# Result stores of a fused attention and max-out kernel: from SyncE's DMA queue to GpSimd's

## The chip, the cores and the metric

The kernel runs on one core of one Trainium2 chip. The time is the device time of one execution, in microseconds (us), from the start of the program to its end. A change of 0.2% of it is 1.2 us.

The engines are named as in the profile: PE is TensorE (its matmuls; PEld its weight loads), DVE is VectorE, ACT is ScalarE, POOL is GpSimd, SP is SyncE, which here issues DMA transfers only. SPq stands for SP's instructions that issue transfers. All engines run side by side, each in the order of its own instruction list, and wait for one another through semaphores.

## The reference

Linear attention over 8 batches of 8 heads (576 rows, head size 64), and a max-out feed-forward over its result (4608 rows of 512, inner size 768), all in float32:

```python
q_s = softmax(q, axis=-1);  k_s = softmax(k, axis=2)      # the reference writes them out
kv  = np.einsum('bhsd,bhse->bhde', k_s, v)
x   = np.einsum('bhsd,bhde->bhse', q_s, kv)               # then rows of all heads side by side: 4608 x 512
h   = np.maximum(np.maximum(x @ w1, x @ w2), x @ w3)
out = h @ w_out
```

## The kernel before

A float32 product is made of three products of two-part operands (a high part and a rest), all summed in PSUM. A chunk is 512 rows of x. Chunk 0 goes through plain products. After it the chunks are taken in pairs, c = 1, 3, 5 and 7 (chunk 7 is paired with the leftover 64 rows of all batches), and a pair goes through seven products P1 to P7 in place of eight (Strassen's scheme in Winograd's form) in both layers.

The first layer of a pair (class `Duo`, `products`, PE L1393) runs over nine units u; a unit's order on PE is P1, P5, P4 of the unit before, P6, P2, P3, P7, each six matmuls of 512 columns. Three things pass between a unit's products through ACT: the copy of P1's sum into a second PSUM bank (`seeded`, L1448), which P6 and P2 add to; the copy of P5's sum into the SBUF tile s5 (L1441, `s_166` in instruction lists), after which P3 may start in P5's bank; and the copy of P6's sum into u2 (L1441, `u_167`), after which P7 may start. The weights of a product come by a transfer of 256 KB each (tiles ws, L1360).

The second layer of a pair (`second`, PE L1581) leaves, for each of v = 0 and 1, four result tiles of 128x512 (function `rows`): two are copied to a tile m of a pool of three (`alone`, L1606), two are summed in place (`added`, DVE L1611) in tiles that the next pair needs again. These are s6 and s7 (`s_164`, `s_165`) and s5 and u2. So the first layer of the next pair (c + 2) waits for stores of this pair: the copy into s5 and the copy into u2 of its unit 0 wait until the stores of these tiles have landed; and one of its seven operands, xb[3] (`xb_123`, cast by ACT at L1323), lies over s6 and waits for the store of s6. Each result is stored by one transfer of 256 KB: the inner function `store`, L1599.

The operands of a pair are made by ACT and DVE (L1323, L1325, L1329), now and then by POOL. POOL also sums weights (`mix_of`, L1235, tiles bd and bdf; L1247) and makes maxima over the partitions (L776, a custom instruction).

All instructions are recorded by one planner (class `Streams`) in a fixed sequence, the table `ORDER`. Each word names a stream and, with a letter, an engine; its step is appended to the instruction list of the engine that issues it. So a step's place among the instructions of its engine is fixed by its place in the table. Semaphore waits are added from the data that instructions share. A transfer takes the next of eight semaphores of its kind in turn and waits for the one that had it before. The program reserves 256 bytes of each SBUF partition as scratch for transfers whose descriptors software writes (L1965, `dynamic_dma_scratch_size=256`); the kernel before issues none such: all its transfers go through SP's queue, except one of ACT.

Of the kernel before, what the change touches and what calls it, by code (L numbers as in the profile page):

```python
# [156 lines left out]
def dve(n):  # L157
    return (n + 68) / 960
# [10 lines left out]
def act_psum(n):  # L169
    return n / 1300 + 0.086  # L170
# [154 lines left out]
def linear_attention_then_maxout_ffn(  # L325
# [29 lines left out]
    nc = tc.nc  # L355
    B, H, S, D = 8, 8, 576, 64
# [930 lines left out]
    class Duo:  # L1287
# [299 lines left out]
        def rows(self, v):  # L1587
            c, bank = self.c, self.bank
            s1, s5v = self.s1[v], self.s5[v]

            def copied(on, f, after, gives, take=()):
                yield Step("A", act_psum(CH), after, gives=("Y2", c, gives, v) if gives else None, take=take, rank=-1000.0)
                if take:
                    bank[on] = pf.tile([P, CH], F32, name="pf")
                    nc.scalar.copy(out=bank[on], in_=f)
                else:
                    nc.scalar.copy(out=f, in_=bank[on])

            def store(h, r, o, free=()):  # L1599
                yield Step("S", 0.42, kb=(128, 2048), gives=("out", c, r, h, v), free=free, rank=-1000.0)  # L1600
                nc.sync.dma_start(out=out_turned[c - 1 + h, 2 * v + r], in_=o)

            def alone(on, h, r, after, free):
                yield Step("A", act_psum(CH), after, take=[("tmp", (c, "y", v, r))], free=[free], rank=-1000.0)
                o = tmp.tile([P, CH], F32, name="m")
                nc.scalar.copy(out=o, in_=bank[on])  # L1606
                yield from store(h, r, o, [("tmp", (c, "y", v, r))])

            def added(on, f, r, after, gives, free=()):
                yield Step("V", dve(CH), after, gives=("Y2", c, gives, v), free=free)  # L1610
                nc.vector.tensor_tensor(out=f, in0=bank[on], in1=f, op=ALU.add)  # L1611
                yield from store(1, r, f)

            y = lambda i: ("pf", (c, "y", i + v))
            return [
                copied(("a", v), s1, [("Y", c, "P1", v), *self.room_s], "s1"),
                copied(("c", v), s5v, [("Y", c, "P5", v), ("out", c - 2, 1, 1, v) if c >= PAIRED else None], "s5"),
                alone(("a", v), 0, 0, [("Y", c, "P2", v), ("Y2", c, "s1", v)], y(0)),
                copied(("b", v), s1, [("Y2", c, "s1", v)], "seed", take=[y(4)]),
                copied(("b", v), s1, [("Y", c, "P6", v)], "u2"),  # L1620
                added(("b", v), s5v, 1, [("Y", c, "P7", v), ("Y2", c, "s5", v)], "c22"),
                added(("c", v), s1, 0, [("Y", c, "P3", v), ("Y2", c, "u2", v)], "c12", [y(2)]),
                alone(("b", v), 0, 1, [("Y", c, "P4", v)], y(4)),
            ]
# [222 lines left out]
    for c, ch in enumerate(chunks):  # L1847
        r = GATES_AT + 100.0 * c
# [11 lines left out]
    for n, d in enumerate(duos):  # L1860
        r = GATES_AT + 100.0 * (PAIRED + 2 * n)
# [18 lines left out]
    for n, d in enumerate([*duos, first]):  # L1880
        r = GATES_AT + 100.0 * (PAIRED + 2 * n)
# [97 lines left out]
```

## Time and profile before

| What | Value |
|---|---|
| Median of 3 runs | 610.97 us (610.48 to 611.84) |
| The profiled execution's own time | 610.54 us |
| Its span, first to last instruction | 608.7 us |
| PE busy | 599.1 us, 98% |
| DVE, ACT, POOL busy | 462.6, 352.1, 62.8 us |
| Result stores by L1601, 256 KB each | 32 on SP's queue |

The span leaves out 1.8 us of the profiled execution, ahead of the first instruction and behind the last. An engine's busy time says how much of the span it had an instruction under way; issuing a transfer is not counted as busy. The rows below give, for one place in the program, when each engine's instructions ran and what ended an idle time before them.

### The profile page before, as it was taken

The numbers are of one execution on the slowest core, as the hardware profiler recorded it, in microseconds if no ns is written. First come the engines' busy times: TensorE is split into PE (matmuls) and PEld (weight loads), VectorE is DVE, ScalarE is ACT, GpSimd is POOL, SyncE is SP. The second block draws the span as 40 slices with busy tenths as digits, with TensorE's granted clock in tenths as the row PEclk, the third lists the DMA queues.
The fourth block names the chain that finished last, engine by engine and source line by source line (L and its number), as shares of the span: only waits on it lengthen the run. The fifth ranks groups of instructions, "written<-read, shape, count | busy, mean of one in ns | idle before, by whom it ended". The sixth has DMA issues, their size and how long they took to land.

```text
span 608.7 us, 9795 instructions
## 1 busy us (share of the span) xinstructions
PE 599.1 (98%) x3359; PEld 482.8 (79%) x3359; DVE 462.6 (76%) x673; ACT 352.1 (58%) x881; POOL 62.8 (10%) x53
## 2 busy tenths in 40 slices
PE   6999999999999999999999999999999999999997
PEld 6688778778878777888787778888878788888886
DVE  8999999989999999955776987376558753242683
ACT  5999968776665696763664874222435641223271
POOL 1201212011201412300020000100010010000000
PEclk9999999999999999999999999999999999999999
DMA  8987789899899999999899846779777266666534
GB/s 318 403 315 248 284 296 367 252 305 320 287 303 326 350 292 278 349 301 294 304 269 303 259 117 204 222 202 288 214 200 226 88 188 191 190 211 214 148 96 146
DMA packets 67408, 154.75 MB, mean 254 GB/s; under 512 B 7712, under 2 KB 18592, under 8 KB 63776
## 3 DMA queue, kind: packets, MB, share of 16 engines
q1 hardware_dynamic: 67216, 154.07, 77.7%
q8 instruction: 27, 0.44, 0.3%
q14 instruction: 21, 0.17, 0.1%
q10 hardware_dynamic: 144, 0.07, 0.0%
HBM read 109.28 MB, written 37.75 MB: 242 GB/s over the span
## 4 chain that ended last, share of the span: by engine, by line
PE 95%; DVE 4%; DMA 1%; issue 0%; ACT 0%
PE pf L1393 50%; PE pf L1581 19%; PE pf L1096 15%; PE pf L1169 3%; PE pa L798 3%; PE pa L1005 2%; DVE qm L848 1%; DMA ident<-in_unit_matrix_dram 1%; PE sm L823 0%; PE pa L934 0%; DVE km L719 0%; DVE wx L587 0%; DVE wx L580 0%; DVE qe L866 0%; PE pa L978 0%; DVE qs L889 0%
## 5 line engine op out<-in xcount | busy, mean ns | idle before, releaser
L1393 PE MATMUL pf<-xb,ws 128*128 128x512 f32 x1134 | 259.9, 390 | 0.0
L1393 PEld LDWEIGHTS pf<-xb,ws 128*128 128x128 f32 x1134 | 212.4, 188 | 44.4
L1096 PE MATMUL pf<-x,wa 128*128 128x512 f32 x408 | 99.2, 396 | 0.0
L1096 PEld LDWEIGHTS pf<-x,wa 128*128 128x128 f32 x408 | 75.4, 188 | 18.6 <-issue 2.1
L1427 DVE TENSOR_TENSOR mm<-pf,mm 128x512 f32<-128x512 f32 x44 | 30.0, 686 | 61.6 <-PE pf L1393 61.4
L1448 ACT COPY pf<-pf 128x512 f32<-128x512 f32 x32 | 18.3, 572 | 93.3 <-PE pf L1393 87.5
L876 ACT ACTIVATE qt<-qt,qm 128x64 f32<-128x64 f32 x162 | 54.1, 338 | 3.6 <-DVE qm L872 2.1
L1441 ACT COPY u<-pf 128x512 f32<-128x512 f32 x27 | 15.8, 587 | 41.3 <-PE pf L1393 38.6
L876 ACT ACTIVATION_READ_ACCUMULATOR qt<-qt,qm 128x1 f32 x162 | 30.8, 190 | 0.0
L1518 DVE TENSOR_TENSOR mm<-mm 128x512 f32<-128x512 f32 (+1 forms) x32 | 29.9, 951 | 0.2
L776 POOL PARTITION_ALL_REDUCE kma<-km x12 | 14.4, 1199 | 138.4 <-DVE km L772 114.4
L1581 PE MATMUL pf<-op_a,oh 128*128 128x512 f32 x84 | 25.9, 389 | 0.0
L1581 PE MATMUL pf<-mix,so 128*128 128x512 f32 x84 | 25.3, 397 | 0.0
L1441 ACT COPY s<-pf 128x512 f32<-128x512 f32 x27 | 15.9, 587 | 15.8 <-PE pf L1393 14.3
L1323 ACT CAST xb<-xf 128x1024 fp32r<-128x1024 f32 x18 | 18.8, 1052 | 9.6 <-DVE xf L1329 6.0
L1433 DVE TENSOR_TENSOR mm<-pf,u 128x512 f32<-128x512 f32 x9 | 6.2, 690 | 21.4 <-PE pf L1393 21.4
L1325 DVE TENSOR_TENSOR xb<-xf,xb 128x1024 fp32r<-128x1024 f32 x16 | 19.9, 1251 | 3.0 <-ACT xb L1323 3.0
L1606 ACT COPY m<-pf 128x512 f32<-128x512 f32 x16 | 9.4, 585 | 18.7 <-PE pf L1581 18.7
L1581 PEld LDWEIGHTS pf<-mix,so 128*128 128x128 f32 x84 | 15.8, 188 | 3.7
L1581 PEld LDWEIGHTS pf<-op_a,oh 128*128 128x128 f32 x84 | 15.8, 188 | 3.3
L1514 DVE TENSOR_TENSOR op_a<-mm,op_a 128x1024 fp32r<-128x1024 f32 (+1 forms) x14 | 13.7, 983 | 5.4 <-ACT op_a L1512 5.4
L798 PEld LDWEIGHTS pa<-vt,kt 128*64 128x64 f32 x480 | 14.7, 137 | 3.2 <-issue 2.1
(248 smaller groups left out, 1126.8 us busy)
## 6 DMA issues: line engine op xcount, KB each, us to landing
ws<-keep_s SPq DMA_DIRECT2D x108, 256.0 KB, 3.9
ws<-keep_a SPq DMA_DIRECT2D x81, 256.0 KB, 3.7
wst<-in_w_dram SPq DMA_DIRECT2D x12, 1024.0 KB, 7.4
keep_a<-wa SPq DMA_DIRECT2D x9, 1024.0 KB, 6.6
so<-keep_t SPq DMA_DIRECT2D x24, 384.0 KB, 4.0
vt<-in_v_rows_dram SPq DMA_DIRECT2D x24, 325.0 KB, 5.6
kt<-in_k_rows_dram SPq DMA_DIRECT2D x12, 640.0 KB, 5.9
keep_s<-mix SPq DMA_DIRECT2D x7, 1024.0 KB, 6.5
```

Source lines behind the costliest of these rows:

```text
L798: nc.tensor.matmul(out=kv[r, i * P : i * P + NV], lhsT=kt[:, i + 2 * hh, s, :], rhs=p.vt[:, hh, s, :], start=(s == 0), stop=(s == 4),)
L876: nc.scalar.activation(out=rows3[:, s, :], in_=rows3[:, s, :], func=AF.Exp, bias=qm[:, s : s + 1], accum_out=qs[:, s : s + 1],)
L1096: nc.tensor.matmul(out=ps, lhsT=wa[i][j // 2][:, j % 2, cc, hl], rhs=r, start=(cc == 0 and t == 0), stop=(cc == NC - 1 and t == 2),)
L1169: nc.tensor.matmul(out=po, lhsT=l, rhs=r[:, j, :], start=(j == 0 and i == 0), stop=(j == NJ - 1 and i == 2))
L1323: nc.scalar.copy(out=xb[i][:, 0], in_=src)
L1325: unit[e].tensor_tensor(out=xb[i][:, 1], in0=src, in1=xb[i][:, 0].bitcast(F32), op=ALU.subtract)
L1393: nc.tensor.matmul(out=bank[on], lhsT=w[:, k, a], rhs=self.operand(p, b, k), start=(i == 0 and p in ("P1", "P5")), stop=(i == 5), skip_gro ...
L1427: nc.vector.tensor_max(out=m, in0=bank[on], in1=m)
L1441: nc.scalar.copy(out=temps()[t], in_=bank[on])
L1448: nc.scalar.copy(out=bank[sb], in_=bank["a"])
L1518: nc.vector.tensor_tensor(out=o[:, parts[k]], in0=x[:, parts[k]], in1=y[:, parts[k]], op=ALU.subtract)
L1581: nc.tensor.matmul(out=bank[on], lhsT=w, rhs=to[k][b][:, kk - k], start=(kk == 0 and i == 0 and not need), stop=(kk == NK - 1 and i == 2), ...
```

## The change

Of the 32 stores at L1601, the 24 of the pairs c = 1, 3 and 5 are issued by POOL (`nc.gpsimd`) on its own DMA queue; the 8 of the last pair, c = 7, stay on SP. The planner's step keeps its engine "S" and its place in `ORDER`.

```diff
             def store(h, r, o, free=()):
                 yield Step("S", 0.42, kb=(128, 2048), gives=("out", c, r, h, v), free=free, rank=-1000.0)
-                nc.sync.dma_start(out=out_turned[c - 1 + h, 2 * v + r], in_=o)
+                q = nc.gpsimd if c < B - 1 else nc.sync
+                q.dma_start(out=out_turned[c - 1 + h, 2 * v + r], in_=o)
```

On POOL, between the second layer of pair 1 and the first of pair 3 (bd and bdf are sums of weights, xb an operand of pair 3, kma the maxima; ISA switches POOL's library; out_dram is the result). The line of the store is 1602 in the changed file:

```order
 L776 ISA kma<-km 128x256 x2
+L1602 DMA out_dram<-m 128x512
 L1235 ISA
 L1235 TENSOR_TENSOR bd_207<-bd_207 128x2x128 x3
+L1602 DMA out_dram<-s_164 128x512
+L1602 DMA out_dram<-s_166 128x512
+L1602 DMA out_dram<-u_167 128x512
 L1325 TENSOR_TENSOR xb_126<-xf_113,xb_126 128x1024
 L1235 TENSOR_TENSOR bdf<-bdf 128x2x128 x2
```

Three stores of pair 1, those of s6, s5 and u2, now stand one behind the other on POOL, behind three sums of weights, and ahead of an operand's rest xb. On SP, the same place of the program (keep_s and ws are weights, vt and qt inputs of a later batch):

```order
 L1360 DMA ws_148<-keep_a_168 128x512
-L1601 DMA out_dram<-m 128x512
 L685 DMA vt_1191<-in_v_rows_dram 128x650
 L1270 DMA keep_s_183<-mix 128x2048
-L1601 DMA out_dram<-s_164 128x512
-L1601 DMA out_dram<-s_166 128x512
 L1360 DMA ws_149<-keep_s_182 128x512
 L1360 DMA ws_150<-keep_s_182 128x512
 L1360 DMA ws_151<-keep_a_169 128x512
-L1601 DMA out_dram<-u_167 128x512
 L705 DMA qt<-in_q_rows_dram 128x1152
```

The four stores are gone from SP's list, and the loads behind them move up. On POOL, between pairs 3 and 5 (qt are the queries of a later batch):

```order
+L1602 DMA out_dram<-s_164 128x512
+L1602 DMA out_dram<-u_167 128x512
+L1602 DMA out_dram<-s_166 128x512
+L1602 DMA out_dram<-m 128x512
 L882 ISA
 L882 TENSOR_TENSOR qt<-qt,qm_264 128x1152
```

Here four stores of pair 3 stand in a row, and a library switch and an operation on queries come behind them. ACT's, DVE's and PE's lists keep their order.

## Rows read from the trace of the kernel before

**Rows 1.** The page: span, each engine's busy time, and the last chain.
```profile
span 608.7 us, 9795 instructions
PE 599.1 (98%) x3359; PEld 482.8 (79%) x3359; DVE 462.6 (76%) x673; ACT 352.1 (58%) x881; POOL 62.8 (10%) x53
PE 95%; DVE 4%; DMA 1%; issue 0%; ACT 0%
```

**Rows 2.** Waits of PE, first and last of four: us in total, times, longest.
```profile
PE sm L524 <- DMA ident<-in_unit_matrix_dram: 4.0, 1, 4.0
...
PE pf L823 <- DMA v<-in_v_first_dram: 0.3, 1, 0.3
```

**Rows 3.** The chain in order of time: start, us, what.
```profile
244.74 1.36 PE pf L1393 x6
246.09 2.48 PE pa L798 x80
248.58 47.82 PE pf L1393 x210
...
374.42 73.44 PE pf L1393 x324
```

**Rows 4.** ACT's timeline: start, us, what [idle before <-what ended it].
```profile
247.58 1.05 ACT L1323 CAST xb<-xf 128x1024 fp32r<-128x1024 f32 x1 [0.29 <-DMA out_dram<-s]
248.54 0.57 ACT L1448 COPY pf<-pf 128x512 f32<-128x512 f32 x1
...
251.65 0.58 ACT L1441 COPY s<-pf 128x512 f32<-128x512 f32 x1
...
252.65 0.59 ACT L1441 COPY u<-pf 128x512 f32<-128x512 f32 x1
...
375.19 0.57 ACT L1441 COPY s<-pf 128x512 f32<-128x512 f32 x1
```

**Rows 5.** POOL's timeline from 226 us on.
```profile
227.94 1.88 POOL L776 PARTITION_ALL_REDUCE kma<-km  x1 [11.88 <-DVE km L772]
241.03 4.10 POOL L1235 TENSOR_TENSOR bd<-bd 128x256 f32<-128x256 f32 x3 [11.21 <-DMA bd<-keep_w]
254.26 2.57 POOL L1325 TENSOR_TENSOR xb<-xf,xb 128x1024 fp32r<-128x1024 f32 x1 [9.13 <-PE pf L1393]
...
312.80 2.94 POOL L778 TENSOR_TENSOR kt<-kt,kma 128x1280 f32<-128x1280 f32 x1 [7.46 <-DMA qT<-tb]
324.32 1.08 POOL L776 PARTITION_ALL_REDUCE kma<-km  x1 [8.58 <-issue]
383.79 2.12 POOL L882 TENSOR_TENSOR qt<-qt,qm 128x1152 f32<-128x1152 f32 x1 [58.38 <-DVE qm L872]
```

**Rows 6.** SP's timeline: the stores (L1601) at pairs 1 to 3.
```profile
235.38 0.38 SPq L1601 DMA_DIRECT2D out_dram<-m  x1
...
240.47 1.26 SPq L1601 DMA_DIRECT2D out_dram<-s  x2
```

**Rows 7.** SP's timeline: the first store (L1601) of the row after pair 3.
```profile
365.57 0.34 SPq L1601 DMA_DIRECT2D out_dram<-s  x1
```

**Rows 8.** L1601, issue to landing, us: whole span, 234 to 246, 480 to 492.
```profile
DMA to landing us min/median/max: 2.0/3.6/8.2
...
DMA to landing us min/median/max: 6.7/7.1/8.2
...
DMA to landing us min/median/max: 2.0/2.0/4.6
```

**Rows 9.** Stretches: length, busy of PE, PEld, DVE, ACT, POOL; clock, DMA share, GB/s.
```profile
242.00:250.00 8.00, 8.00 (x105) 6.70 (x104) 7.96 (x7) 6.18 (x8) 3.05 (x2) 1.00 1.01 380
250.00:258.00 8.00, 8.00 (x37) 6.63 (x36) 7.45 (x10) 5.18 (x12) 3.26 (x2) 1.00 0.97 348
...
364.00:372.00 8.00, 8.00 (x37) 6.52 (x36) 6.57 (x8) 3.37 (x5) 0.00 (x0) 1.00 0.62 213
```

## The prediction

> **What bounds the kernel now.** I read the page first, then the waits of PE, then the chain of work, and then, at the places where stores hand tiles to the next pair, the timelines of the engines. PE is busy for 599.1 of 608.7 us, and the chain that ended last runs along PE for 95% of the span [rows 1]. PE waits four times in all, the longest 4.0 us for the first transfer of the program, and none of its waits is for an instruction of the pairs [rows 2]. From the end of the first stage on, one matmul follows the other: in the first layer of pair 3, 210 matmuls take 47.82 us, 0.2277 us each [rows 3]. So nothing that makes a transfer or a queue quicker can shorten the run, and whatever makes PE wait once, from pair 1 on, lengthens it by that wait. The question is how much slack the stores' landings have.
>
> **The tightest handover, pair 1 to pair 3.** The six matmuls of P1 of unit 0 start at 244.74, P5 starts at 248.58 [rows 3]. With 6 x 0.2277 = 1.37 us for a product, P6 starts at 249.95, P2 at 251.31, P3 at 252.68 and P7 at 254.04. Against these stand ACT's times. The cast at 247.58 had idled for the landing of a store of an s tile: that is operand xb[3], which lies over s6. Directly behind it, in ACT's order, comes the copy at L1448 that P6 adds to; it ends at 249.11 [rows 4]. So P6 has 0.84 us of slack against the store of s6. The copy into s5 ends at 252.23 against P3 at 252.68, the copy into u2 at 253.24 against P7 at 254.04 [rows 4]. Counted back by the copies' 0.58 and 0.59 us, the stores must have landed by:
> - s6: the cast may start at 248.42 at the latest, 0.84 after 247.58,
> - s5: 252.68 - 0.58 = 252.10,
> - u2: 254.04 - 0.59 = 253.45.
>
> **What the change removes.** 24 issues leave SP. In the rows an issue takes 0.34 to 0.38 us [rows 6, 7], some 8 us in all, and the loads behind the stores move up. That is work off the path: PE waits for no weight anywhere [rows 2]. Value: nothing, and it can't be more, since PE's waits of 5.8 us lie in the first stage, before the first store.
>
> **What it adds, term one: place in the queue.** SP issued the store of s6 at 240.47 [rows 6]. On POOL it stands behind the three sums bd, which start at 241.03, when their load has landed, and take 4.10 us [rows 5]. The store can start at 245.13 at the earliest, 4.66 us later than before. Its landing on SP's queue took 7.1 us at the median of this stretch against 2.0 in a calm one [rows 8], because the DMA engines are busy to 1.01 and 0.97 of their time [rows 9] and a transfer stands behind all that SP issued before it. On a queue of its own it does not stand behind those.
>
> **Term two: what a store costs POOL (g).** No row shows POOL issuing a transfer. Bounds: below, SP's issue, 0.34 us [rows 7]; above, POOL's longest operation after the stores begin, 2.94 us [rows 5]. I take 1.1 us, the row of the custom instruction kma, 1.08 us [rows 5], as that too is a short piece of software on POOL. [...]
>
> **Term three: the flight (f), from the end of the issue to landing.** Below: 2.0 - 0.34 = 1.7 us, a calm stretch. Above: 7.1 - 0.34 = 6.8, a place behind SP's backlog [rows 8]. On a queue of its own, 256 KB at half of 348 GB/s take 1.5 us and at all of it 0.75 [rows 9]; so I take the calm one and 0.8 more, 2.5 us.
>
> **Term four: one by one, or overlapping.** Three stores stand in a row behind the sums: s6, s5, u2. On SP two were issued within 1.26 us and were in flight together [rows 6]. Whether POOL can do that, no row shows. The program leaves 256 bytes of a partition for transfers that software describes, and a store has 128 rows; I take it that a second does not fit, and a store is issued when the one before has landed. The two ends are thus: overlapping, each g = 1.1 after the other, or one by one, each g + f = 3.6 after the other. [...]
>
> **The sum at this handover.** One by one, from 245.13: s6 lands at 248.73, s5 at 252.33, u2 at 255.93. Against the limits: s6 makes the cast start at 248.8, 0.4 late; s5 is 0.2 late; u2 is 2.5 late. Waits of one chain don't add, the largest counts: PE loses 2.5 us, at P7 of unit 0 of pair 3. In general, with C = g + f, the loss is 245.13 + 3C - 253.45 = 3C - 8.32. The first m store adds to it at most: it now goes out at 229.82, behind kma (227.94 + 1.88) [rows 5], ahead of the load of bd and not at 235.38 [rows 6]; 256 KB at 348 GB/s are 0.75 us by which the sums could start late. I leave that for the range.
>
> **The other handovers.** Pair 3 to 5: POOL has s6, u2, s5 in a row from 365.57 [rows 7] and no sums ahead. The flight is nearer to the calm one (DMA share 0.62 [rows 9]): C = 2.8 and s5 lands at 374.0. P3 of unit 0 starts at 374.42 + 2 x 1.37 = 377.15 [rows 3], ACT takes its copy at 375.19 [rows 4], the limit is 377.15 - 0.57 = 376.6. No loss below C = 3.67. Pair 5 to 7: the stores' data come spread out, and in the calm stretch [rows 8] each is away before the next; no loss. Behind the stores on POOL: xb waited for PE until 254.26 [rows 5]; u2's issue ends at 245.13 + 2 x 3.6 + 1.1 = 253.43, ahead of it. The queries' operation at 383.79 waited for DVE [rows 5]; four stores from 365.57 and a library switch (8.58 us, the idle time before kma at 324.32 after L778 [rows 5]) end at 365.57 + 3 x 2.8 + 1.1 + 8.58 = 383.65, just in time. The first m store and the switch behind it end at 229.82 + 1.1 + 8.58 = 239.5, before bd's 241.03. DVE's and ACT's orders are the same.
>
> **Forecast: slower by 2.5 us.** Against the profiled execution 610.54 + 2.5 = 613.0 us; the median of the runs shown is 0.43 above that execution, so 613.5 us. Chance 0.58, with its own range of C from 3.2 to 4.3: 3.2 gives +1.3; 4.3 (g = 1.1 and the flight of all stores' median, 3.6 - 0.4) gives +4.6 here and 365.57 + 3 x 4.3 - 376.6 = +1.9 at pair 5, +6.5 together.
>
> **Rivals.**
> - *No measurable change: the stores overlap, or are quick.* Overlapping with g = 1.1 and f = 2.5, s5 and u2 land at 249.8 and 250.9, in time, and only s6 costs 0.4 us: 611.4. With g + f below 3.2 nothing is late at all: 611.0. For it: SP overlaps its stores, and 245.13 + 3.2 still meets the 248.42. Against it: the 256 bytes. It decides on that side as soon as s6 lands by 249.4 and u2 by 254.6. [...] Chance 0.28.
> - *Slower by another way: the stores overlap, but s6 is slow.* If the own queue gets no better place than SP's (f = 6.8), s6 lands at 245.13 + 1.1 + 6.8 = 253.0, and P6 waits 4.6 us: 615.6. Or a first issue on POOL takes long: from g = 2.6 on, the library switch behind the m store makes bd late, by g - 2.6. Chance 0.10.
> - *Faster.* SP's stores held up its loads (the store at 240.47 waited for data). Only if a load were late for PE would that pay, and PE waits for none [rows 2]: at most some tenths, 610.5. Chance 0.04.
>
> **How the numbers follow.** 0.2% of 610.97 is 1.2 us, about what a measurement of this kernel can tell from no change. Slower by more: 0.58 + 0.10 = 0.68; within: 0.28; faster: 0.04. The range goes from 610.9 (nothing is late) to 618.3 (C = 4.3 with the sums 0.75 late: 6.5 + 0.75 over 610.97).
>
> **What would show each step.** The chain around 250 us should show PE waiting: first a few tenths at P6 for ACT L1448, then over 2 us at P7 for ACT's copy into u2, itself waiting for the landing of the u tile's store. POOL's timeline should show the three stores of 245 us and later each some 3.6 us after the other, with 1.1 us of work. If they stand 1.1 us apart, term four is wrong, and the first rival holds; if PE waits at P6 alone, the flight is the cause. If PE also waits near 377 us, C is above 3.7. The forecast is wrong as a whole if the sums bd end earlier or if P6's slack of 0.84 us is not what ACT's order makes it.

## The result, and the profile after

The changed kernel takes 616.41 us at the median of 5 runs (615.6 to 617.23), the kernel before 610.97 us: 5.4 us more, a ratio of 1.0089 with a 95% interval of 1.0074 to 1.0104. The forecast was 613.5 us, its range went to 618.3 us: the direction is the forecast one, the loss is more than twice as large. Two executions below lay far off, one of the kernel before (2123 us) and one with PE's wait filled (752 us, mean clock 0.754), and are left out of the ratios and of that kernel's median.

The page of the changed kernel, first the span and the engines, then the DMA queues (packets, MB, share of 16 engines); it answers to [rows 1]:

```profile
span 614.8 us, 9797 instructions
...
PE 601.5 (98%) x3359; PEld 483.5 (79%) x3359; DVE 464.5 (76%) x673; ACT 352.1 (57%) x881; POOL 76.7 (12%) x77
...
q1 hardware_dynamic: 63760, 147.78, 73.9%
q0 software_dynamic: 1920, 6.29, 2.7%
```

The span grew by 6.1 us, PE's busy time by 2.4. Both matter: PE waits more, and it also works longer on the same 3359 matmuls. q0 is POOL's queue, 24 stores of 80 packets each. POOL's own 14 us more are the issues, off the path: on POOL, unlike SP, the profile counts an issue as busy time (77 instructions are 53 and 24 stores).

The waits of PE in the changed kernel, which answer to [rows 2] (us in total, times, longest):

```profile
PE pf L1393 <- ACT u L1441: 2.8, 2, 2.0
...
PE pf L1393 <- ACT pf L1448: 0.2, 1, 0.2
```

These are the two that the prediction named, P6 behind the copy at L1448 and P7 behind the copy into u2, and one that it did not name: the second wait for a copy into u2, 0.7 us near 319 us. ACT's timeline at the handover from pair 1 to pair 3 answers to [rows 4]:

```profile
248.78 1.05 ACT L1323 CAST xb<-xf 128x1024 fp32r<-128x1024 f32 x1 [2.35 <-DMA qt<-in_q_rows_dram]
249.73 0.58 ACT L1448 COPY pf<-pf 128x512 f32<-128x512 f32 x1
...
252.48 0.59 ACT L1441 COPY s<-pf 128x512 f32<-128x512 f32 x1
...
256.18 0.58 ACT L1441 COPY u<-pf 128x512 f32<-128x512 f32 x1 [2.59 <-DMA out_dram<-u]
```

The cast starts 1.2 us later than before, the copy into s5 0.8, the copy into u2 3.5 us. (The first bracket names a load of qt; what the cast needs is s6's landing at 248.75, as the chain below shows.) POOL's timeline there answers to [rows 5]:

```profile
239.48 2.39 POOL L1235 TENSOR_TENSOR bd<-bd 128x256 f32<-128x256 f32 x3 [8.38 <-DMA bd<-keep_w]
241.81 0.74 POOL L1602 DMA_DIRECT2D out_dram<-s  x1
249.07 0.55 POOL L1602 DMA_DIRECT2D out_dram<-s  x1 [6.52 <-DVE xb L1325]
252.71 0.55 POOL L1602 DMA_DIRECT2D out_dram<-u  x1 [3.09 <-PE pf L1393]
257.79 2.37 POOL L1325 TENSOR_TENSOR xb<-xf,xb 128x1024 fp32r<-128x1024 f32 x1 [4.54 <-ACT xb L1323]
```

The three stores of the row stand 7.3 and 3.6 us apart, though one costs POOL only 0.55 to 0.74 us. The brackets name an operation of DVE on an operand and a matmul, which no store needs; the stores' data had long been there (DVE's sums into s6, s5 and u2 end by 241.53). What POOL really waited for is seen in the chain in order of time (start, us, what), where a transfer counts from its issue to its landing:

```profile
241.81 6.95 DMA out_dram<-s
...
249.07 0.55 POOL out_dram L1602
...
252.71 3.39 DMA out_dram<-u
...
256.18 0.59 ACT u L1441
...
256.82 5.29 PE pf L1393 x15
```

s6's store lands at 248.75 and the next is issued 0.32 us later. u2's lands at 256.10, and 0.08 us later ACT copies. The last row tells where PE's extra work is: 15 matmuls in 5.29 us are 0.353 us each, against 0.2277 [rows 3]. Two stretches of the changed kernel show why (length, busy of PE, PEld, DVE, ACT, POOL; granted clock, DMA share, GB/s):

```profile
253.00:257.00 4.00, 1.96 (x9) 1.24 (x8) 2.10 (x4) 1.41 (x4) 0.26 (x1) 1.00 0.91 310
257.00:261.00 4.00, 4.00 (x11) 3.13 (x12) 2.56 (x4) 1.20 (x2) 3.05 (x2) 0.57 0.75 238
```

PE was idle for half of the first 4 us. In the next 4 us it was busy all the time, but the granted clock was 0.57 at the mean: from 258 to 260 us it was 0.50. So 11 matmuls went through; in the same 4 us of the kernel before, at a clock of 1.00, 19 did.

Compared matmul by matmul with the kernel before, PE is 0.4 us later from P6's first matmul on, 0.1 more from its second, 2.25 more at P7 (2.74 together), 1.6 more behind it by the clock, and 1.1 more at the wait near 319 us. What is left of the span's 6.1 us comes in steps of 0.3 us and less.

At the handover from pair 3 to pair 5 the stores are late for nobody (POOL's timeline, which answers to [rows 7]):

```profile
371.82 0.55 POOL L1602 DMA_DIRECT2D out_dram<-s  x1 [29.48 <-DVE s L1612]
374.42 0.54 POOL L1602 DMA_DIRECT2D out_dram<-u  x1 [2.06 <-DVE s L1612]
377.05 0.54 POOL L1602 DMA_DIRECT2D out_dram<-s  x1 [2.08 <-ACT m L1607]
```

They stand 2.6 us apart. The landings of L1602 from 234 to 246 us and from 366 to 382 us, which answer to [rows 8] (us from issue, min, median, max):

```profile
DMA to landing us min/median/max: 6.9/6.9/6.9
...
DMA to landing us min/median/max: 2.3/2.3/3.5
```

### The profile page after: what moved, and what is told of

Read it like the earlier page. It is cut to its first block, busy times and chain, and to the rows that moved or that the text cites. A ratio compares the mean times of both kernels' runs of the same rounds, so it can differ in the third digit from the quotient of the medians.

```text
span 614.8 us, 9797 instructions
## 1 busy us (share of the span) xinstructions
PE 601.5 (98%) x3359; PEld 483.5 (79%) x3359; DVE 464.5 (76%) x673; ACT 352.1 (57%) x881; POOL 76.7 (12%) x77
## 4 chain that ended last, share of the span: by engine, by line
PE 86%; DMA 5%; DVE 4%; issue 1%; SPq 1%; ACT 1%; POOL 0%; POOLq 0%; ACTq 0%; DVEq 0%
PE pf L1393 47%; PE pf L1581 15%; PE pf L1096 15%; PE pf L1169 3%; PE pa L798 2%; PE pa L1005 2%; DMA qt<-in_q_rows_dram 1%; DMA out_dram<-s 1%; DMA bd<-keep_w 1%; SPq L914 1%; DMA vt<-in_v_rows_dram 1%; ACT qt L876 1%; DVE qm L848 1%; DMA out_dram<-u 1%; DMA ident<-in_unit_matrix_dram 0%
## 5 line engine op out<-in xcount | busy, mean ns | idle before, releaser
L1448 ACT COPY pf<-pf 128x512 f32<-128x512 f32 x32 | 18.3, 573 | 93.7 <-PE pf L1393 84.2
L776 POOL PARTITION_ALL_REDUCE kma<-km x12 | 16.9, 1410 | 143.0 <-DVE km L772 114.7
L1518 DVE TENSOR_TENSOR mm<-mm 128x512 f32<-128x512 f32 (+1 forms) x32 | 32.7, 1037 | 0.2
L872 DVE TENSOR_REDUCE qm<-qt 128x18 f32<-128x1152 f32 x11 | 14.8, 1346 | 4.6 <-DMA qt<-in_q_rows_dram 4.6
L778 DVE TENSOR_TENSOR kt<-kt,kma 128x1280 f32<-128x1280 f32 x11 | 16.3, 1482 | 2.2 <-POOL kma L776 2.2
```

The source lines that it names most:

```text
L776: nc.gpsimd.partition_all_reduce(kma, km, P, bass_isa.ReduceOp.max)
L1448: nc.scalar.copy(out=bank[sb], in_=bank["a"])
L1518: nc.vector.tensor_tensor(out=o[:, parts[k]], in0=x[:, parts[k]], in1=y[:, parts[k]], op=ALU.subtract)
```

## The experiments

The theory after the result: one store of POOL fills the scratch, so the three go one by one; the first is slow because the DMA engines are full; u2's lands late, PE idles at P7, and because it idled its clock falls for some microseconds. Rivals: another cause of the queueing, of the slow first store, of the fall of the clock, or of the wait near 319 us. Each kernel ran beside the kernel before on the same chip; "lost" below is the median less the median of the kernel before there.

| Kernel | Median, us | Lost, us | Ratio, 95% interval |
|---|---|---|---|
| changed kernel again | 616.59 | 5.8 | 1.0080 to 1.0106 |
| 384 bytes of scratch | 612.35 | 1.6 | 1.0018 to 1.0053 |
| 512 bytes of scratch | 611.93 | 1.2 | 1.0012 to 1.0040 |
| 512 bytes, s6 of pair 1 on SP | 611.56 | 1.0 | 1.0007 to 1.0025 |
| only pairs 3 and 5 on POOL | 611.14 | 0.4 | 0.9998 to 1.0017 |
| only pair 1 on POOL | 615.71 | 5.0 | 1.0068 to 1.0109 |
| u2 of pair 1 on SP | 613.37 | 2.6 | 1.0033 to 1.0073 |
| 1 MB less ahead of the row | 616.27 | 5.6 | 1.0073 to 1.0101 |
| changed, PE's wait filled with work | 615.52 | 4.8 | 1.0071 to 1.0097 |
| before, PE delayed by work | 613.15 | 2.4 | 1.0026 to 1.0052 |
| before, PE delayed by idling | 614.80 | 4.0 | 1.0054 to 1.0078 |

**Which stores cost.** Only the stores of pairs 3 and 5 on POOL, and the other half, only those of pair 1:

```diff
-                q = nc.gpsimd if c < B - 1 else nc.sync
+                q = nc.gpsimd if c in (3, 5) else nc.sync
```

> Only the stores of pairs 3 and 5 on POOL, those of pair 1 back on SP. Theory (all of the loss starts at the handover from pair 1 to pair 3, the slip near 314 us too, which follows from it): 611.0 us, PE without a wait after the first stage. Rival 1 (the slip near 314 us comes from something else, such as SP's shorter list further on): 612.3 us. Rival 2 (the stores of pairs 3 and 5 cost on their own, in POOL's time or at the handover to pair 5): over 612 us with a wait of PE near 377 us.

```diff
-                q = nc.gpsimd if c < B - 1 else nc.sync
+                q = nc.gpsimd if c == 1 else nc.sync
```

> The other half: only the stores of pair 1 on POOL, those of pairs 3 and 5 on SP. Theory: 616.4 us as the changed kernel, with PE's waits near 250 and 254 us, the clock level of 0.5 behind the second, and the slip near 314 us. Rival (the later stores on POOL cost part of the 5.4 us): by that part less, under 615 us; the later stores save something: over 617 us. If the two halves add, this run's loss and that of the run with pairs 3 and 5 make 5.4 us.

Pairs 3 and 5 lose 0.4 us, at the limit of the measurement; pair 1 loses 5.0. They add up to the 5.4 us of the change. That the 0.4 us are the stores' is not shown: with pairs 3 and 5 on POOL, PE waits once after the first stage, 0.2 us near 325 us, and for a load of weights; in the kernel before with PE delayed by work (below), with no store on POOL, it waits there too, 0.4 us. The waits of PE in the kernel with pair 1 alone:

```profile
PE pf L1393 <- ACT u L1441: 2.5, 1, 2.5
...
PE pf L1393 <- ACT pf L1448: 0.4, 1, 0.4
PE pf L1393 <- ACT s L1441: 0.4, 1, 0.4
```

The same places, and P3 besides, since s5's store landed later here (253.2 for 252.4). But in this profiled execution the clock stays full (1.00 from 254 to 266 us), and there is no wait near 319 us. What the profile of the changed kernel shows is thus not in every execution.

**The room.** More scratch, nothing else (the second edit lays four small tiles into one, since 96 bytes of a partition were lacking):

```diff
-    nc = _bacc.Bacc("TRN2", target_bir_lowering=False, num_devices=1, dynamic_dma_scratch_size=256)
+    nc = _bacc.Bacc("TRN2", target_bir_lowering=False, num_devices=1, dynamic_dma_scratch_size=384)
```

> The changed kernel with 384 bytes of scratch in place of 256, nothing else. Theory (a store of POOL fills the scratch, so the next one is issued only when it has landed, and PE's wait at P7 of pair 3 and the clock level of 0.5 behind it follow from that): two stores now fit, s5's store goes out within 1 us of s6's, u2's about 0.5 us after s6's landing (near 249.3), lands by 253, PE waits under 0.5 us at P7 and keeps its clock. Of the 5.4 us lost, 2.25 and 1.6 come back: 611.4 to 612.7 us, by whether the slip of 1.3 us near 314 us stays. Rival 1 (POOL's queue carries one store at a time whatever its scratch): 616.4 us, stores as before. Rival 2 (two in flight share the way, and s6's lands the later for it): P6 waits for the cast of xb[3], over 1 us more there, 613.5 us or more.

```diff
-    ones = const.tile([P, 1], F32, name="ones")
-    zero = const.tile([P, 1], F32, name="zero")
-    warm = const.tile([P, 1], F32, name="warm")
+    one = const.tile([P, 8], F32, name="ones")
+    ones, zero = one[:, 0:1], one[:, 1:2]
+    warm = one[:, 2:3]
...
-    adder = const.tile([P, 2], I32, name="adder")
+    adder = one[:, 4:6].bitcast(I32)
...
-    nc = _bacc.Bacc("TRN2", target_bir_lowering=False, num_devices=1, dynamic_dma_scratch_size=256)
+    nc = _bacc.Bacc("TRN2", target_bir_lowering=False, num_devices=1, dynamic_dma_scratch_size=512)
```

> The changed kernel with 512 bytes of scratch (the 96 bytes of a partition that this lacks come from four small tiles laid into one). Theory (a store takes more than half of 256 bytes, and 512 hold three): s6's, s5's and u2's stores go out within 2.5 us of one another, all land by 250, PE waits for none of them, full clock: 611.0 us, in the bounds of the kernel before. Rival 1 (three in flight with SP's loads hold one another up, s6's among them): P6 or P3 wait, 612 us or more. Rival 2 (384 bytes already held all that can be in flight): u2's store waits for s6's landing again, 612.3 us as with 384.

POOL's timeline with 384 bytes:

```profile
241.04 1.36 POOL L1602 DMA_DIRECT2D out_dram<-s  x2
247.74 0.54 POOL L1602 DMA_DIRECT2D out_dram<-u  x1 [5.34 <-issue]
```

and with 512:

```profile
241.48 1.30 POOL L1602 DMA_DIRECT2D out_dram<-s  x2
242.77 0.55 POOL L1602 DMA_DIRECT2D out_dram<-u  x1
```

With 384 bytes two stores go out together and u2's waits until s6's has landed (247.43); with 512 all three go out within 1.3 us. That is what the theory said, but for u2's landing with 512 bytes, at 250.74 and not by 250; and rival 1 falls: the queue does carry several. In both profiled executions PE waits for no store. Yet 1.6 and 1.2 us stay lost at the median, with 512 bytes where 0.3 had been expected: the executions reach from 611.03 to 616.05 us, and the slowest of them has a mean clock of 0.996, as where PE idles.

**What is left with 512 bytes.** One store back on SP:

```diff
-                q = nc.gpsimd if c < B - 1 else nc.sync
+                q = nc.gpsimd if c < B - 1 and not (c == 1 and o is s6) else nc.sync
```

> The kernel with 512 bytes of scratch, and one store of 24 back on SP: that of s6 of pair 1. With 512 bytes 1.2 us were still lost at the median, and the executions spread from 611.03 to 616.05 us. Theory (s6's store, behind the sums bd on POOL, landed at 248.12 in the profiled execution against 248.42, the latest time that costs nothing, so that other executions miss it): with its place on SP its landing is near 247.5 again, and the loss and the spread go: 611.0 us at the median. Rival (the rest of the loss comes from another place, such as s5's and u2's stores or loads held up by the stores of POOL): 611.9 us and the spread as before.

The spread is smaller (611.02 to 612.81 us), which points to s6's store behind the sums as what made single executions slow; with 11 and 12 executions this is not shown. The median is 611.56 us, where 611.0 had been expected, and stays 1.0 us above the kernel before. In the profiled execution PE loses 0.5 us of it near 314 us, at the wait for a copy into u2 that is taken up below. The rest is not found.

**The last of the row alone.**

```diff
-                q = nc.gpsimd if c < B - 1 else nc.sync
+                q = nc.gpsimd if c < B - 1 and not (c == 1 and o is u2) else nc.sync
```

> The changed kernel with one store of 24 back on SP: that of u2 of pair 1, the last of the three in a row. Theory (the row of three, one by one, makes u2 late): s6 still lands near 248.8 and s5 near 252.5 to 253.2, so P6 starts 0.4 to 0.7 us late and P3 none to 0.7, and P7 waits for nothing more: 0.4 to 1.4 us lost, 611.4 to 612.4 us, clock at its full level. Rival (u2's store is late wherever it is issued, behind SP's loads or because its data come late): P7 waits 2 us, 615 us or more.

P7 waits for nothing of its own any more, as the theory said; but more is lost than it said, 2.6 us. In the profiled execution s5's store, now the last of the row, lands at 253.21, P3 is 1.0 us late behind 0.2 us at P6, and two of the eight executions have the low mean clock (0.996 and 0.994) and take 616.8 and 617.3 us.

**Why the first store is slow.** A transfer of 1 MB that SP issues ahead of it is put elsewhere (this kernel leaves out unit 1's own weights):

```diff
-            nc.sync.dma_start(
-                out=keep_s[u].rearrange("p r c k t n -> p (r c k t n)"),
+            for to in {8: (8, 1), 1: ()}.get(u, (u,)): nc.sync.dma_start(
+                out=keep_s[to].rearrange("p r c k t n -> p (r c k t n)"),
```

> The changed kernel, 256 bytes of scratch, with one transfer of SP of 1 MB (L1270 to keep_s of unit 1, issued at 238.06 ahead of s6's store) put some 30 us earlier, where it takes the values of unit 8 in place of its own. Theory (s6's store takes 6.2 us because the DMA engines have 7 us of transfers before them when it is issued, whatever queue it comes on): 1 MB at 357 GB/s less is 2.9 us less, s6's store lands 2 to 3 us earlier against its issue (3.3 to 4.2 us of flight), the row behind it moves up by that, u2 lands near 253.3, and PE's waits shrink from 3 to 4.2 us to under 1: 611 to 612 us. Rival (the flight of the first store of a row is POOL's own, by its software or the sums before it): 6 us of flight again, 616.4 us.

POOL's timeline of this kernel, and the landings of L1602 from 234 to 250 us:

```profile
239.95 4.61 POOL L1235 TENSOR_TENSOR bd<-bd 128x256 f32<-128x256 f32 x3 [8.69 <-DMA bd<-keep_w]
244.52 0.74 POOL L1602 DMA_DIRECT2D out_dram<-s  x1
249.04 0.55 POOL L1602 DMA_DIRECT2D out_dram<-s  x1 [3.77 <-issue]
```

```profile
DMA to landing us min/median/max: 2.8/3.5/4.2
```

s6's store takes 4.2 us from its issue in place of 6.95, and the rival, 6 us again, falls. The 2.75 us less are close to 1 MB at 357 GB/s, 2.9; but the store also starts 2.7 us later, and SP issues nothing from 241.0 us on until 246.2, so that more of its other loads have moved by then. This run does not part the two.

The trace of the changed kernel shows the load itself. Between the end of the store's issue and 245.8 us, only SP's queue moves (packets, MB, share of the engines):

```profile
q1 hardware_dynamic: 433, 1.10, 97.7%
```

and two of SP's loads of 256 KB, weights issued at 238.9 and 240.0, take still longer than the store from issue to landing:

```profile
DMA to landing us min/median/max: 8.5/8.7/8.9
```

So the first store is slow because the DMA engines are full of what SP issued before; the queue of its own let it pass only part of that. A rival that no run tests is that DVE's sums of SBUF tiles, which run without a break from 241.6 us on in both kernels, delay POOL's store, as POOL's sums took longer beside them (last section). SP's loads, as slow with no part of POOL's in them, make it needless.

The time of the run, though, did not move, and the expectation of 611 to 612 us failed: the three sums ahead of the store took 4.61 us instead of 2.39, so that the store started 2.7 us later and landed at the same 248.7. One of the three ran for 2.97 us beside DVE's sums of operands.

**The clock.** Ten products with zeros in PE's wait, in the changed kernel; then eleven at the same place of the kernel before, where there is no wait; then the kernel before with ACT's copy into u2 made seven times:

```diff
                 for i, (k, a, b) in enumerate(terms):
+                    for _ in range(10 if (c, p, u, i) == (3, "P3", 0, 5) else 0):
+                        nc.tensor.matmul(
+                            out=bank[on][:, 0:P], lhsT=ident, rhs=zero.broadcast_to([P, P]),
+                            start=False, stop=False, skip_group_check=True,
+                        )
```

> The changed kernel with ten products of 128 columns with zeros (0.21 us each, 2.1 us, they add nothing to the sums) ahead of the last matmul of P3 of unit 0 of pair 3, so that PE works where it waited 2 us for the copy into u2. The wait itself can't get shorter. Theory (the clock fell to 0.5 because PE had idled): the granted clock stays at its full level there, and 1.6 us come back: 614.8 us, or 613.5 if the slip near 314 us goes with it. Rival (the clock falls for another reason, whatever PE does in these 2 us): the level of 0.5 stands at the same place, 616.4 us. A second rival (the products delay the end of P3 and with it DVE or ACT): over 616.4 us.

> The kernel before, with eleven products of 128 columns with zeros (0.21 us each, they add nothing to the sums) ahead of the last matmul of P3 of unit 0 of pair 3: PE is made 2.3 us later at 254 us by work, with no store on POOL. Theory (PE's clock falls after it has idled, not after a delay as such): full clock, 610.7 + 2.3 = 613.0 us. If the slip of 1.3 us near 314 us is a consequence of any delay: 614.3 us.

```diff
-                nc.scalar.copy(out=temps()[t], in_=bank[on])
+                [nc.scalar.copy(out=temps()[t], in_=bank[on]) for _ in range(7 if (c, u, t) == (3, 0, 0) else 1)]
```

> The kernel before, with ACT's copy into u2 of unit 0 of pair 3 made seven times over instead of once (the same values, some 0.48 us each, so that the last ends near 256.1): PE is made about 2.0 us later at 254 us by idling, with no store on POOL. Theory (idling makes the clock fall): the granted clock falls to 0.5 behind the wait for 3 to 4 us in most executions, 610.7 + 2.0 + 1.6 = 614.3 us. Rival (the fall comes of the transfers of POOL or of another thing in the changed kernel): full clock, 612.7 us.

Stretches of the kernel before with PE delayed by work (columns as above):

```profile
253.00:257.00 4.00, 4.00 (x31) 3.71 (x30) 1.42 (x3) 1.23 (x2) 3.18 (x2) 1.00 0.93 349
257.00:261.00 4.00, 4.00 (x20) 3.29 (x19) 3.01 (x5) 1.57 (x8) 0.76 (x2) 1.00 0.84 226
```

and of the kernel before with PE delayed by idling:

```profile
253.00:257.00 4.00, 1.42 (x7) 0.84 (x5) 1.61 (x3) 3.81 (x8) 0.00 (x0) 1.00 0.96 363
257.00:261.00 4.00, 3.96 (x10) 3.16 (x11) 2.64 (x3) 1.43 (x2) 2.98 (x2) 0.57 0.60 184
```

No store is on POOL in either. Where PE worked, the clock stays full in all five executions (mean 0.999 to 1.0), and the loss is the 2.4 us of the work. Where it idled, 2.6 us in the profiled execution, the same stretch of 0.57 follows, and four of five executions have a mean clock of 0.996 or 0.997. In the profiled execution PE is 2.9 us late at P7 and 1.7 more behind it; the median of the loss is 4.0 us. This settles it for these executions: the clock fell because PE had idled.

In the changed kernel with the wait filled, the clock is full in all four executions that were compared (mean 0.999 to 1.0), but the time fell by 0.9 us only against 616.4, where 1.6 were expected. In its profiled execution s6's store was issued at 242.55, 0.7 later than in the changed kernel and ahead of any added product, and u2's landed at 257.76 for 256.10; PE still waited 0.3 and 0.5 us for the copies. So by its time alone this run is inconclusive.

**The changed kernel again**, and the wait near 319 us:

> The changed kernel once more, unchanged, for a second profile and five more times. Theory: 616.4 us at the median, PE's waits for the landings between 3 and 4.2 us in all, the clock at 0.5 for 3 to 4 us behind the wait at P7 in most executions. The slip of 1.1 us near 314 us, for which no cause has been shown: absent again if it is the variation of one execution, there again if it belongs to the change.

The waits of PE in the second profile of the changed kernel:

```profile
PE pf L1393 <- ACT u L1441: 2.0, 1, 2.0
PE pf L1393 <- ACT s L1441: 1.1, 1, 1.1
```

and the stretch behind them:

```profile
258.00:262.00 4.00, 4.00 (x13) 3.05 (x12) 2.55 (x4) 0.93 (x2) 3.06 (x2) 0.58 0.67 179
```

PE loses 3.5 us here in all by the landings and 1.6 by the clock, and nothing near 319 us. In the first profile ACT's copy into u2 was late there because its activations of queries, ahead of it, waited for DVE's maxima and these for a load of SP. From its issue to its landing that load (L705) took, in the changed kernel and then in its second profile:

```profile
DMA to landing us min/median/max: 8.8/8.8/8.8
```

```profile
DMA to landing us min/median/max: 5.3/5.3/5.3
```

It takes 6.0 us in the kernel before, 7.6 in the one with PE delayed by work, where no store is on POOL, 5.4 in the one delayed by idling, and 8.0 with 512 bytes and s6 on SP. So its flight varies from execution to execution, and in two of the three profiles where it took over 7 us, PE waits for the copy near 314 to 319 us (not in the one with PE delayed by work). Over the two profiles of the changed kernel it is there once. Whether the change makes it more frequent is open.

## Why the prediction was half right

**What bounds the kernel: right.** PE's list is the path. Work of 2.3 us put into it cost 2.4, and transfers on another queue saved nothing.

**Place in the queue: wrong by 3.3 us.** s6's store was to start at 245.13 and started at 241.81. The load of bd landed earlier, and the three sums took 2.39 us instead of the 4.10 of [rows 5]. The prediction had named this as what would make it wrong.

**g: half of what was taken**, 0.55 to 0.74 us at this handover (0.87 for the first store) for 1.1, inside the bounds. An issue on POOL took 0.2 to 0.4 us more than one on SP (0.55 to 0.74 against 0.34), and from issue to landing in a calm stretch it is 2.3 against 2.0.

**f: wrong for the first store.** The step "on a queue of its own it does not stand behind those" was the author's estimate and failed for the most part: 6.2 us after the issue (6.95 less 0.74), near the upper bound of 6.8 and not the 2.5 taken, though two of SP's loads beside it took longer still, 8.5 and 8.9 from issue to landing. The two behind it took 2.8 each, and in the calm stretch 1.75 (2.3 less 0.55), as taken. POOL's queue moved nothing for over 3 us while SP's had 97.7% of the 16 engines: for this term the rival in which the own queue gets no better place than SP's (f = 6.8) was the nearer one.

**One by one: right**, and shown by the runs with 384 and 512 bytes. That a second store does not fit into 256 bytes was the author's estimate; the runs show one store of the row under way at a time with 256 bytes, two with 384 and three with 512, and not what one store takes.

**The sum at the handover: right by errors that cancelled.** Predicted landings 248.73, 252.33, 255.93; measured 248.75, 252.40, 256.10. The start was 3.3 us early, the first flight 3.7 us long and g 0.4 to 0.55 short; behind the first, each flight was 0.3 long, and each issue came 0.3 us after the landing before, for which the sum had no term. P6 0.4 late, P7 2.5: measured 0.4 and, all told, 2.74. That the largest lateness counts and not the sum of all holds: u2's store was 2.65 late against its limit of 253.45.

**The other handovers: right.** 2.6 us apart at pair 3 to 5 for the 2.8 taken, no wait of PE.

**What failed is the step "PE loses 2.5 us", as the whole of the loss.** The mechanism was right, and its term too small in two ways.

- The clock. The sum had PE's idle time and, with no reason given, nothing behind it. PE worked the next 4 us at a mean granted clock of 0.57, 1.6 us lost; the mean clock of 7 of the 9 executions of the changed kernel is 0.997 or less. At 7 in 9 that is 1.2 us.
- The flights. One value stood for all executions. In three profiles (two of the changed kernel, and pair 1 alone) PE lost 2.7, 3.5 and 4.2 us by the landings: at the mean 3.5, 1.0 more than the forecast.

Together, as an estimate, 2.5 + 1.2 + 1.0 = 4.7 of the 5.4 us. Of the other 0.7 the run with pairs 3 and 5 has 0.4, and the late load near 319 us 1.1 in one execution of two; these are not resolved further. The rival in which the stores overlap was made by the scratch of 512 bytes: it was priced at 0.4 us lost and measured 1.2.

## What to carry to other kernels

Moving a transfer to an idle engine's queue bought place in that engine's list here, hardly a way of its own to memory: its flight, 6.95 us from issue to landing against 2.3 in a calm stretch, was set for the most part by what SP's queue had given the DMA engines before it. On POOL, ask how many transfers the reserved scratch holds (of these, one with 256 bytes, two with 384, three with 512); with one at a time, a row of three waits three flights, here 6.95, 3.3 and 3.4 us. And a wait of PE of 2.0 to 2.6 us cost, in most executions here, its own length and then some 1.6 us more by the lower clock, so price the idle time together with the stretch behind it.

## What the runs showed of the hardware that had not been expected

- After a wait of PE of 2.0 to 2.6 us, the 4 us behind it had a mean granted clock of 0.57 or 0.58, in three profiles alike, with 10 to 13 matmuls in place of 19 or 20. It doesn't follow every time: with pair 1 alone on POOL, PE waited 2.5 us in the profiled execution and the 4 us behind it had 1.00; with 1 MB less ahead of the row it waited 1.9 us, and the stretch from 254 to 258 us, which holds the wait, had 1.00 for 0.91 in the changed kernel.
- A sum of two SBUF tiles on POOL took 0.75 us beside DVE's sums out of PSUM, and 1.6 to 2.97 us beside DVE's sums of SBUF tiles; these took up to 1.76 us there and 1.21 alone. Near 317 us of the changed kernel's first profile it went the other way: beside an operation of POOL of 2.95 us, two of DVE's between SBUF tiles (L1518) took 4.56 us together, for 1.82 in the kernel before. POOL's three sums at the handover from pair 1 to pair 3 took 4.10 us from 241.03 us on in the kernel before, and 2.39 from 239.48 on in the changed kernel. That the two engines hinder each other is read from these timelines; no run took one of them away.
